# Two mirrored outputs from one weight load in the inverse transform's second stage

## The chip, the cores and the metric

One core of a Trainium2 chip runs the kernel. A NeuronCore has TensorE (PE), which multiplies a moving operand by a loaded weight and writes to PSUM; VectorE (DVE) and ScalarE (ACT), which read PSUM and write SBUF; GpSimd (POOL) and SyncE (SP), which here mostly issue transfers. The engines run side by side, each through its own instructions in order, and wait for each other by semaphores. The metric is the device time of one execution in microseconds.

## The reference

The input `x` is 8 sequences of 5696 steps with 128 channels, and `h` is one filter of the same length for each channel. The first half is a long causal convolution, computed by a Fourier transform of twice the length:

```python
Xf = np.fft.rfft(x, n=2 * S, axis=1)
Hf = np.fft.rfft(h, n=2 * S, axis=0)
y = np.fft.irfft(Xf * Hf[None], n=2 * S, axis=1)[:, :S, :]
```

The second half takes that `y` as its `x` and mixes the steps by two full 5696 x 5696 matrices:

```python
theta = x @ w_theta
zr, zi = x * np.cos(theta), x * np.sin(theta)
y = np.einsum('ts,bsd->btd', w_tok_r, zr) + np.einsum('ts,bsd->btd', w_tok_i, zi)
u = x + y
return u + np.maximum(u @ w_ch, 0.0)
```

## The kernel before

The transform of length 11392 is split into 178 x 64. Work goes in eight groups: a group is two of the sequences and one half (64) of the channels, so 128 rows in all. Each group passes four stages. Stages A and B are the forward transform and the product with the filter's spectrum, stages C and D the inverse.

- Stage A (`stage_a`, line 241): 64 matmuls of 180 columns, weights from `x` (line 250), evicted to `a_` by ACT, in group 0 and 1 in part by DVE (lines 257, 259).
- Stage B (`stage_b`, line 411): 12 chunks. Each is a block of small matmuls (`f2`, line 270), an eviction to `xs` by ACT (line 431), and a product with the filter's spectrum `hs` into `uv_t` by DVE (lines 433, 438). `hs` comes by transfers on SP (line 423), four chunks ahead.
- Stage C (`stage_c`, line 444): 16 chunks of 16 matmuls (lines 453, 454), evicted to `g_` by DVE or ACT (lines 458, 460).
- Stage D (`stage_d`, line 478): for each of 64 output columns n, 89 outputs m: a weight is a slice of `g_`, the moving operand is a slice of a table of cosines and sines, `e_t`, or of its negative, `e_neg`. The time step is 64 m + n. The result goes to `yt`, with m outermost and n innermost, in bf16, and from there to HBM.

In stage D the offset of a column from the middle is v = |n - 32|. For odd v below 28 there are 14 pairs of columns, 32 + v and 32 - v, that use the same four weights; each column of a pair takes four matmuls of 89 columns (`terms_of`, line 463). All other columns take two. That is 184 matmuls a group, in seven chunks of up to ten neighbouring columns (`CHN`, line 90). A chunk has one PSUM tile of two banks, five columns in a bank, and one eviction; chunks 0 and 3 are evicted by DVE (line 493), the other five by ACT (line 495). Columns below 32 read the table backwards (`e[:, ::-1]`, line 476).

All four stages draw their PSUM tiles from one pool of four (`psum`, line 104). The order on PE, DVE, ACT is that in which the program emits the work. A helper, `woven` (line 280), merges lists of chunks by given fractions: stage C of group g with stage A of group g + 1 (line 791), then stage D of group g with stage B of group g + 1 (line 799). In the second mix, D's seven chunks are placed from 0.08 to 1.1 and B's twelve from 0 to 0.8, so that on PE the order is B0 B1 D0 B2 B3 D1 B4 B5 B6 D2 B7 B8 D3 B9 B10 D4 B11 D5 D6. In the last group there is no stage B; five steps of the next phase (`phase_step`, line 736) stand between D's chunks. These steps compute theta, sines and cosines.

After the seventh chunk `yt` is sent off: in groups 0 to 6 by eight transfers on SP (line 502), in the last by POOL, two of them straight into the tile `ya` of the phase steps (line 729). Then come the remaining phase steps, and the mixing by the two large matrices (lines 1200 and 1279), whose weights POOL loads (line 680) and DVE transposes (line 894).

Of the kernel before, what the change touches and what calls it, by code (L numbers as in the profile page):

```python
# [15 lines left out]
AF = mybir.ActivationFunctionType  # L16
# [6 lines left out]
def kernel(  # L23
# [10 lines left out]
    nc = tc.nc  # L34
# [41 lines left out]
    N2 = 64  # L76
    N1 = NF // N2
    NB = S // N2
    K1 = N1 // 2 + 1
    CK = 8  # L80
    HD = D // 2
    EN = N2 // 2 + 1
# [3 lines left out]
    assert N1 * N2 == NF and NB * N2 == S and NB % 2 == 1 and K1 <= P  # L86
    CHK = [(c0, min(CK, K1 - c0)) for c0 in range(0, K1, CK)]
    NCK = len(CHK)
    CN = 10
    CHN = [(c0, min(CN, N2 - c0)) for c0 in range(0, N2, CN)]  # L90
    UVW = 2 * HD * K1
    YP = [(n * S // 4, (n + 1) * S // 4) for n in range(4)]
    NP = 14
    ND = N2 - 2 * NP
    RC = 2 * NP + 2 * ND
# [227 lines left out]
    ps = psum()  # L323
# [136 lines left out]
                nc.vector.tensor_copy(g_out, g_in)  # L460
        return [lambda q=q: chunk(q) for q in range(0, 2 * HD, 8)]

    def terms_of(n):

        v = abs(n - N2 // 2)
        c, s = e_t[:K1, v, 0, :], e_t[:K1, v, 1, :]
        if v % 2 and v < 2 * NP:
            i = v // 2
            c_, s_ = (e_neg[:K1, i, r, :] for r in range(2))
            late = ((s, c_) if n >= N2 // 2 else (s_, c))  # L470
            out_ = [(i, c), (NP + i, s), (RC + i, late[0]), (RC + NP + i, late[1])]
        else:
            f = (n - N2 // 2) % N2
            i = 2 * NP + (f // 2 if f % 2 == 0 else N2 // 2 + (f - 2 * NP) // 2)
            out_ = [(i, c), (ND + i, s)]
        return [(i, e if n >= N2 // 2 else e[:, ::-1]) for i, e in out_]

    def stage_d(st, bp, dh, then=None):
        def chunk(n0, cn):
            if n0 == 0:  # L480
                st["yt"] = fy.tile([P, NB, N2], BF16, tag="yt", name="yt")
            g_, yt = st["g"], st["yt"]
            ps = psum()
            nq = 5 if cn == CN else cn
            for j in range(cn):
                o = ps[:, j // nq, (j % nq) * NB:(j % nq + 1) * NB]
                terms = terms_of(n0 + j)
                for i, (at, e_) in enumerate(terms):
                    nc.tensor.matmul(o, g_[:K1, at, :], e_, start=(i == 0), stop=(i == len(terms) - 1))
            y_out = yt[:, :, n0:n0 + cn].rearrange("p m (a q) -> p m a q", q=nq)  # L490
            y_in = ps[:, :cn // nq, :nq * NB].rearrange("p a (q m) -> p m a q", q=nq)
            if n0 in (0, 3 * CN):
                nc.vector.tensor_copy(y_out, y_in)
            else:
                nc.scalar.activation(y_out, y_in, AF.Copy)
            if n0 + cn == N2:
                if then is not None:
                    then(yt)
                for t0, t1 in [(H, S)] if then else YP:
                    for e in range(2):  # L500
                        with tc.issue_after(sides["row"]) if then else ExitStack():
                            (nc.gpsimd if then else nc.sync).dma_start(
                                yt_hbm[dh * HD:(dh + 1) * HD, 2 * bp + e, t0:t1],
                                yt[64 * e:64 * e + 64].rearrange("p m n -> p (m n)")[:, t0:t1])
        return [lambda n0=n0, cn=cn: chunk(n0, cn) for n0, cn in CHN]

    zz_n, ZB = [0], 3
    groups = [(bp, dh) for bp in range(B // 2) for dh in range(2)]
# [833 lines left out]
```

## Time and profile before

| | us |
|---|---|
| median of three runs | 2044.71 (2043.49 to 2048.08) |
| the profiled execution | 2041.79 |
| its span, first to last instruction | 2040.0 |
| PE busy in the span | 1958.3 (96%) |
| DVE busy | 1538.0 (75%) |
| POOL busy | 967.4 (47%) |
| ACT busy | 640.1 (31%) |
| stage D's matmuls (line 489), one group | 184 instructions |
| stage D's evictions by DVE (line 493) | 16 x 890 elements, 1080 ns each |
| stage D's evictions by ACT (line 495) | 32 x 890 elements, 917 ns each, and 8 x 356, 448 ns |

A row of the profile gives the engine, the line of the kernel, the operation, what it writes and reads, and how often. Lengths overlap: an instruction of PE lasts about 0.2 us from its start to its modelled end, while the next one starts about 0.04 us after it, and an instruction of DVE or ACT starts some 0.1 us before the one ahead of it ends. So the cost of an instruction on a full engine is the distance to the next start, not its length. The granted clock is the share of TensorE's full clock that it was given in a stretch.

### The profile page before, as it was taken

How to read it: one execution, taken by the hardware profiler on the slowest of the kernel's cores; microseconds unless marked ns; L12 is line 12 of the kernel's file. 1: busy time of each engine (PE TensorE's matmuls, PEld its weight loads, DVE VectorE, ACT ScalarE, POOL GpSimd, SP SyncE). 2: the span in 40 equal slices, each digit the busy share in tenths (PEclk: the TensorE clock that was granted, in tenths of full speed). 3: DMA queues.
4: the chain of work that ended last, by engine and by line, in shares of the span. 5: the costliest groups of instructions: out<-in, count | busy, mean ns of one | idle time of the engine just before them, and what ended most of it. 6: DMA issues, size and time to landing. Idle time of an engine off the chain costs nothing.

```text
span 2040.0 us, 42587 instructions
## 1 busy us (share of the span) xinstructions
PE 1958.3 (96%) x16297; PEld 1080.5 (53%) x16297; DVE 1538.0 (75%) x2817; ACT 640.1 (31%) x936; POOL 967.4 (47%) x1769
## 2 busy tenths in 40 slices
PE   7899898889999999999999998999999999999998
PEld 5788897644444444444444443444444444444444
DVE  7878887657778787878776767867777786777767
ACT  6888887853233323233200000011111111111111
POOL 8324313374454545453666454453545545354450
PEclk8899999899999999999999999999999999999999
DMA  9999989899898989898999798796978869788793
GB/s 155 158 164 155 168 161 244 256 251 189 143 181 172 180 169 167 177 178 171 173 168 145 132 262 199 108 153 127 153 137 140 152 124 157 130 148 144 135 156 84
DMA packets 510349, 334.77 MB, mean 164 GB/s; under 512 B 186631, under 2 KB 463111, under 8 KB 510055
## 3 DMA queue, kind: packets, MB, share of 16 engines
q0 software_dynamic: 322368, 157.47, 60.6%
q1 hardware_dynamic: 181792, 163.03, 27.3%
q10 hardware_dynamic: 5984, 11.54, 1.6%
q8 instruction: 128, 2.10, 0.4%
q14 instruction: 77, 0.63, 0.1%
HBM read 374.82 MB, written 95.24 MB: 230 GB/s over the span
## 4 chain that ended last, share of the span: by engine, by line
PE 66%; DVE 3%; DMA 2%; issue 1%; POOL 1%; ACT 0%; DVEq 0%; ACTq 0%; SPq 0%
PE m L1279 61%; DVE c L1286 1%; DMA ring<-in_moe_w_tok_r_dram 1%; PE utp L974 1%; PE v L981 1%; PE m L1283 1%; POOL ring L680 1%; DVE b L835 1%; PE m L1166 1%; DVE wt L894 1%; DMA b<-z_hbm 1%; PE theta_ps L564 0%; PE tpz L922 0%; PE m L1200 0%; DMA zl<-zl_hbm 0%
## 5 line engine op out<-in xcount | busy, mean ns | idle before, releaser
L680 POOL DMA_DIRECT2D ring<-in_moe_w_tok_i_dram x720 | 388.5, 545 | 656.0 <-DVE wt L894 575.4
L680 POOL DMA_DIRECT2D ring<-in_moe_w_tok_r_dram x720 | 387.1, 545 | 142.9 <-DVE wt L894 83.9
L894 DVE STREAM_TRANSPOSE wt<-ring 128x384 f32<-128x384 f32 (+2 forms) x720 | 359.7, 526 | 124.6 <-PE m L1279 80.3
L1279 PE MATMUL m<-b,wt 128*128 128x512 bf16 x1640 | 389.7, 380 | 1.9 <-DVE wt L894 1.7
L1279 PEld LDWEIGHTS <-wt 128*128 128x128 bf16 x1804 | 176.3, 98 | 219.7 <-DVE wt L894 7.9
L1286 DVE TENSOR_TENSOR c<-c,m 128x512 f32<-128x512 f32 x412 | 266.4, 672 | 0.4 <-PE m L1279 0.4
L976 ACT ACTIVATE ring<-utp 128x512 bf16<-128x512 bf16 x85 | 50.8, 598 | 581.8 <-PE utp L974 581.8
L1200 PE MATMUL m<-b,wt 128*128 128x512 bf16 x480 | 113.7, 387 | 9.6 <-DMA b<-zz 3.9
L453 PE MATMUL ps<-r_u,uv_t 128*128 128x128 f16 x1024 | 118.5, 222 | 4.2 <-DVE uv_t L438 1.9
L454 PE MATMUL ps<-r_v,uv_t 128*128 128x100 f16 x1024 | 116.4, 210 | 0.1
L971 ACT ACTIVATE ub<-c 128x512 bf16<-128x512 f32 x88 | 55.2, 630 | 193.7 <-DVE c L1241 114.9
L153 POOL DMA_DIRECT2D x<-in_x_dram x128 | 99.3, 781 | 20.9 <-POOL x L151 14.9
L454 PEld LDWEIGHTS <-uv_t 128*128 128x128 f16 x1024 | 101.3, 99 | 4.6 <-issue 3.3
L453 PEld LDWEIGHTS <-uv_t 128*128 128x128 f16 x1024 | 101.6, 99 | 2.5 <-DVE uv_t L438 2.0
L433 DVE TENSOR_TENSOR uv_t<-xs,hs 128x2048 f16<-128x2048 f16 x77 | 91.2, 1223 | 14.2 <-ACT xs L431 9.4
L431 ACT ACTIVATE xs<-ps 128x1024 f16<-128x1024 f32 x96 | 90.6, 974 | 24.1 <-PE ps L270 11.0
L1200 PEld LDWEIGHTS <-wt 128*128 128x128 bf16 x528 | 51.1, 99 | 69.3 <-issue 11.0
L566 ACT ACTIVATE red<-theta_ps,magic 128x512 f32<-128x512 f32 (+1 forms) x46 | 31.7, 689 | 154.9 <-PE theta_ps L564 96.0
L270 PEld LDWEIGHTS <-w_t 64*128 64x128 f16 x3240 | 55.3, 97 | 27.1 <-issue 20.0
L924 ACT ACTIVATE ring<-tpz 128x512 bf16<-128x512 bf16 (+1 forms) x46 | 27.5, 598 | 132.2 <-PE tpz L922 118.2
L250 PE MATMUL ps<-f_t,x 89*128 89x180 f16 x512 | 65.9, 262 | 1.7 <-DVE a L257 1.6
L835 DVE TENSOR_TENSOR b<-b 128x1024 bf16<-128x1024 bf16 x100 | 61.4, 684 | 0.0
(2925 smaller groups left out, 3755.1 us busy)
## 6 DMA issues: line engine op xcount, KB each, us to landing
ring<-in_moe_w_tok_r_dram POOLq DMA_DIRECT2D x352, 96.0 KB, 4.5
ring<-in_moe_w_tok_i_dram POOLq DMA_DIRECT2D x352, 96.0 KB, 4.9
ring<-in_moe_w_tok_r_dram POOLq DMA_DIRECT2D x352, 80.0 KB, 4.5
ring<-in_moe_w_tok_i_dram POOLq DMA_DIRECT2D x352, 80.0 KB, 3.8
cp_hbm<-c SPq DMA_DIRECT2D x88, 256.0 KB, 2.6
c<-cp_hbm SPq DMA_DIRECT2D x88, 256.0 KB, 4.6
out_dram<-c SPq DMA_DIRECT2D x88, 256.0 KB, 4.2
hs<-hf_hbm SPq DMA_DIRECT2D x77, 256.0 KB, 3.7
```

The source lines that it names most:

```text
L153: nc.gpsimd.dma_start(x16[p0:p1, e, n0:n0 + 16, :HD], bass.AP(tensor=src.tensor, offset=src.offset + (p0 * N2 + n0) * D + dh * HD, ap=[[N2 ...
L250: nc.tensor.matmul(ps[:, i // 2, (i % 2) * 2 * K1:(i % 2 + 1) * 2 * K1], lhs(q + i), f1_t[:NB], start=True, stop=True)
L431: nc.scalar.activation(xs[:, :, :, :ck], ps, AF.Copy)
L433: nc.vector.tensor_tensor(uv[:, :, :, c0:c0 + ck], xs.rearrange("p e d k -> p e (d k)").unsqueeze(1).to_broadcast([P, 2, 2, HD * CK]), hv. ...
L453: nc.tensor.matmul(o, u_t[:, at:at + P], r_u, start=True, stop=False)
L454: nc.tensor.matmul(o[:, 2 * NP:], v_t[:, at:at + P], r_v, start=False, stop=True)
L680: nc.gpsimd.dma_start(wb[32 * i:32 * i + 32, :ng, :nj * 64], bass.AP(tensor=a.tensor, offset=a.offset + row0 * S + p * H + i * QR + j0 * 6 ...
L835: return [lambda f=f, x=x: f(*x) for f, x in ((nc.vector.tensor_sub, (bt[M3], b12, b22)), (nc.vector.tensor_sub, (bt[M4], b21, b11)), (nc. ...
L894: nc.vector.transpose(wt.rearrange("p j t r -> p (j t r)").bitcast(F32).rearrange("p (j g t) -> p g j t", j=TJ, g=4)[:, :ng, :nj], wb[:, : ...
L1200: nc.tensor.matmul(ms[n // 2 * 2 + h], a[n][:, j, :, r], bts_of[p][jj][n % 2 * 2 + h][:, r, :], start=(n % 2 == 0 and jj == 0 and r == 0), ...
L1279: nc.tensor.matmul(ms[q], a[q][:, j, :, r], bts[jj][q][:, r, :], start=(jj == 0 and r == 0), stop=(jj == NJ - 1 and r == 1 and q not in left))
L1286: nc.vector.tensor_tensor(c, z, ms[q], op=op)
```

## The change

The chunks of stage D are no longer neighbouring columns. `D_TILES` lists seven chunks, each with the columns of its two banks and its evictions:

- three chunks of ten even columns (0 to 18, 20 to 38, 40 to 58), as singles;
- two chunks of four pairs, and one of four pairs with the single columns 1 and 3;
- a last one with two pairs and the single columns 60 to 63.

A pair is a negative item. Its four matmuls have 178 moving columns each: for the two shared terms the same block of the table twice (a broadcast), for the two others a block and its counterpart, elsewhere in the table. The lower column of a pair then comes out with m backwards, and its eviction writes `yt` backwards (`kind` 2). Each chunk of pairs has one eviction for the upper columns and one for the lower. Singles below 32 still read the table backwards.

A group then has 72 matmuls of 89 columns and 56 of 178, and 13 evictions in place of 7: DVE has chunk 0 (890 elements) and chunk 3 (two of 356), ACT the others (two of 890, five of 356, three of 178). The chunks' places in the order are as before.

```diff
-    def terms_of(n):
-        v = abs(n - N2 // 2)
-        c, s = e_t[:K1, v, 0, :], e_t[:K1, v, 1, :]
-        if v % 2 and v < 2 * NP:
-            i = v // 2
-            c_, s_ = (e_neg[:K1, i, r, :] for r in range(2))
-            late = ((s, c_) if n >= N2 // 2 else (s_, c))
-            out_ = [(i, c), (NP + i, s), (RC + i, late[0]), (RC + NP + i, late[1])]
...
-        return [(i, e if n >= N2 // 2 else e[:, ::-1]) for i, e in out_]
+    def terms_of(item):
+        if item < 0:
+            i = ~item
+            c, s, c_, s_ = 4 * i + 2, 4 * i + 3, 2 * EN + 2 * i, 2 * EN + 2 * i + 1
+            same = [e_blk[:K1, b:b + 1, :].to_broadcast([K1, 2, NB]) for b in (c, s)]
+            return [(i, same[0]), (NP + i, same[1]), (RC + i, e_blk[:K1, s:s_ + 1:s_ - s, :]),
+                    (RC + NP + i, e_blk[:K1, c_:c - 1:c - c_, :])]
...
+    def even(k, by_dve):
+        n0 = 4 * 5 * k
+        return [list(range(n0, n0 + 10, 2)), list(range(n0 + 10, n0 + 20, 2))], [(by_dve, 0, 2, 0, 5, 0, n0, 2)]
+
+    def pairs_of(k, by_dve, more=()):
+        i = 4 * k
+        banks = [[~i, ~(i + 1), *more[:1]], [~(i + 2), ~(i + 3), *more[1:]]]
+        return banks, [(by_dve, 0, 2, 0, 2, 1, H_ + 1 + 2 * i, 2), (by_dve, 0, 2, 0, 2, 2, H_ - 1 - 2 * i, -2),
+                       *([(by_dve, 0, 2, 4 * NB, 1, 0, more[0], 2)] if more else [])]
+
+    D_TILES = [even(0, True), pairs_of(0, False), even(1, False), pairs_of(1, True), pairs_of(2, False, (1, 3)), even(2, False),
+               ([[~12, ~13], list(range(N2 - 4, N2))],
+                [(False, 0, 1, 0, 2, 1, H_ + 25, 2), (False, 0, 1, 0, 2, 2, H_ - 25, -2), (False, 1, 1, 0, 4, 0, N2 - 4, 1)])]
...
     def stage_d(st, bp, dh, then=None):
-            for j in range(cn):
-                o = ps[:, j // nq, (j % nq) * NB:(j % nq + 1) * NB]
-                terms = terms_of(n0 + j)
-                for i, (at, e_) in enumerate(terms):
-                    nc.tensor.matmul(o, g_[:K1, at, :], e_, start=(i == 0), stop=(i == len(terms) - 1))
-            y_out = yt[:, :, n0:n0 + cn].rearrange("p m (a q) -> p m a q", q=nq)
-            y_in = ps[:, :cn // nq, :nq * NB].rearrange("p a (q m) -> p m a q", q=nq)
-            if n0 in (0, 3 * CN):
+            for bank, items in enumerate(banks):
+                at = 0
+                for item in items:
+                    w = 2 * NB if item < 0 else NB
+                    o = ps[:, bank, at:at + w]
+                    if item < 0:
+                        o = o.rearrange("p (h m) -> p h m", h=2)
+                    terms = terms_of(item)
+                    for k, (col, e_) in enumerate(terms):
+                        nc.tensor.matmul(o, g_[:K1, col, :], e_, start=(k == 0), stop=(k == len(terms) - 1))
+                    at += w
+            for by_dve, bank, nb, at, nq, kind, n0, dn in evictions:
+                y_in = ps[:, bank:bank + nb, at:at + nq * NB * (2 if kind else 1)]
+                n1 = n0 + dn * nb * nq
+                y_out = yt[:, ::-1, n0:n1:dn] if kind == 2 else yt[:, :, n0:n1:dn]
...
+                if by_dve:
                     nc.vector.tensor_copy(y_out, y_in)
```

More of the change, by code (lines that the diff above doesn't have):

```diff
@@ L88 @@
     NCK = len(CHK)
-    CN = 10
-    CHN = [(c0, min(CN, N2 - c0)) for c0 in range(0, N2, CN)]
     UVW = 2 * HD * K1
@@ L309 @@
     e_t = e_flat.rearrange("p (n r m) -> p n r m", r=2, m=NB)
+    e_blk = e_all.rearrange("p (b m) -> p b m", m=NB)
     e_f = [e_flat[:K1, 22 * NB * n:22 * NB * (n + 1)].bitcast(F32) for n in range(3)]
@@ L461, in stage_c @@
         return [lambda q=q: chunk(q) for q in range(0, 2 * HD, 8)]
-    def terms_of(n):
-        v = abs(n - N2 // 2)
-        c, s = e_t[:K1, v, 0, :], e_t[:K1, v, 1, :]
-        if v % 2 and v < 2 * NP:
-            i = v // 2
-            c_, s_ = (e_neg[:K1, i, r, :] for r in range(2))
-            late = ((s, c_) if n >= N2 // 2 else (s_, c))
-            out_ = [(i, c), (NP + i, s), (RC + i, late[0]), (RC + NP + i, late[1])]
[L472 to L475, printed above, removed]
-        return [(i, e if n >= N2 // 2 else e[:, ::-1]) for i, e in out_]
+    def terms_of(item):
[5 more added lines that the diff above has]
+                    (RC + NP + i, e_blk[:K1, c_:c - 1:c - c_, :])]
+        v = abs(item - N2 // 2)
+        f = (item - N2 // 2) % N2
+        i = 2 * NP + (f // 2 if f % 2 == 0 else N2 // 2 + (f - 2 * NP) // 2)
+        return [(at, e_t[:K1, v, r, :] if item >= N2 // 2 else e_t[:K1, v, r, ::-1])
+                for r, at in ((0, i), (1, ND + i))]
@@ new lines @@
+    H_ = N2 // 2
+    def even(k, by_dve):
[6 more added lines that the diff above has]
+                       *([(by_dve, 0, 2, 4 * NB, 1, 0, more[0], 2)] if more else [])]
@@ L478, in stage_d, with chunk @@
+    D_TILES = [even(0, True), pairs_of(0, False), even(1, False), pairs_of(1, True), pairs_of(2, False, (1, 3)), even(2, False),
+               ([[~12, ~13], list(range(N2 - 4, N2))],
+                [(False, 0, 1, 0, 2, 1, H_ + 25, 2), (False, 0, 1, 0, 2, 2, H_ - 25, -2), (False, 1, 1, 0, 4, 0, N2 - 4, 1)])]
+    assert NP == 14
     def stage_d(st, bp, dh, then=None):
-        def chunk(n0, cn):
-            if n0 == 0:
+        def chunk(n_, banks, evictions):
+            if n_ == 0:
                 st["yt"] = fy.tile([P, NB, N2], BF16, tag="yt", name="yt")
@@ L483, in chunk @@
             ps = psum()
-            nq = 5 if cn == CN else cn
-            for j in range(cn):
-                o = ps[:, j // nq, (j % nq) * NB:(j % nq + 1) * NB]
-                terms = terms_of(n0 + j)
-                for i, (at, e_) in enumerate(terms):
-                    nc.tensor.matmul(o, g_[:K1, at, :], e_, start=(i == 0), stop=(i == len(terms) - 1))
-            y_out = yt[:, :, n0:n0 + cn].rearrange("p m (a q) -> p m a q", q=nq)
-            y_in = ps[:, :cn // nq, :nq * NB].rearrange("p a (q m) -> p m a q", q=nq)
-            if n0 in (0, 3 * CN):
[L493 to L496, printed above, removed]
+            for bank, items in enumerate(banks):
[13 more added lines that the diff above has]
+                y_out = yt[:, ::-1, n0:n1:dn] if kind == 2 else yt[:, :, n0:n1:dn]
+                y_out = y_out.rearrange("p m (a q) -> p m a q", q=nq)
+                if kind:
+                    y_in = y_in.rearrange("p a (q h m) -> p m a q h", h=2, m=NB)[:, :, :, :, kind - 1]
+                else:
+                    y_in = y_in.rearrange("p a (q m) -> p m a q", m=NB)
+                if by_dve:
+                    nc.vector.tensor_copy(y_out, y_in)
+                else:
+                    nc.scalar.activation(y_out, y_in, AF.Copy)
+            if n_ + 1 == len(D_TILES):
                 if then is not None:
@@ L504, in chunk @@
                                 yt[64 * e:64 * e + 64].rearrange("p m n -> p (m n)")[:, t0:t1])
-        return [lambda n0=n0, cn=cn: chunk(n0, cn) for n0, cn in CHN]
+        return [lambda n_=n_, t=t: chunk(n_, *t) for n_, t in enumerate(D_TILES)]
     zz_n, ZB = [0], 3
```

## The prediction

> **What bounds the kernel now.** I read four views, in this order: the table by stage, the timeline of one group's end, the clock by gate windows, and the groups by line. In each fence below a line of the table by stage is: window, its length, then busy time (and instructions) of PE, PE weight load, DVE, ACT, POOL, the granted clock, DMA.
>
> The stages first. The first two windows are one group of the transform (its D/B stretch, in which stage D of one group is mixed with stage B of the next, then its C/A stretch); the last is all of the mixing.
>
> ```profile
> 201.90:220.00 18.10, 15.47 (x555) 14.32 (x553) 16.47 (x16) 15.12 (x18) 4.88 (x9) 1.00 0.93 152
> ...
> 220.00:237.80 17.80, 17.77 (x313) 17.54 (x312) 13.17 (x12) 15.31 (x21) 8.47 (x16) 1.00 1.28 181
> ...
> 400.00:2040.00 1640.00, 1613.51 (x8505) 766.12 (x8502) 1226.28 (x2434) 325.36 (x531) 813.15 (x1502) 0.99 0.87 161
> ```
>
> The mixing is 1640 of the 2040 us, and the change has no instruction in it. The edited stage lies in eight stretches before 381 us: seven D/B stretches of about 18 us and one last D stretch (366.8 to 381.2 us). In D/B it is DVE that is full (16.47 of 18.10 us), with PE waiting in between; in C/A it is PE (17.77 of 17.80). So whatever D does to PE counts only at the seams of D/B, and in the last stretch, where phase steps take B's place.
>
> The seam is in the timeline (start, length, engine, line, what, count).
>
> ```profile
> 215.72 0.38 PE L270 MATMUL ps<-a__4565,w_t 64*128 64x64 f16 x13 [0.66 <-issue]
> 216.03 1.28 PEld L489 LDWEIGHTS <-g__4578 90*128 90x128 f16 x30
> 216.24 1.08 DVE L493 CAST yt<-ps 128x890 bf16<-128x890 f32 x1
> 217.24 2.36 DVE L433 TENSOR_TENSOR uv_t<-xs,hs 128x2048 f16<-128x2048 f16 x2
> 217.38 0.29 PE L270 MATMUL ps<-a__4565,w_t 64*128 64x64 f16 x8
> 217.49 0.93 ACT L495 ACTIVATE yt<-ps 128x890 bf16<-128x890 f32 x1
> 217.60 1.62 PEld L489 LDWEIGHTS <-g__4578 90*128 90x128 f16 x38
> 218.55 0.41 ACT L431 ACTIVATE xs<-ps 128x256 f16<-128x256 f32 x1
> 219.07 1.27 ACT L495 ACTIVATE yt<-ps 128x890 bf16<-128x890 f32 x2
> 219.17 0.69 PEld L250 LDWEIGHTS <-x 89*128 89x128 f16 x8
> 219.50 0.71 DVE L438 TENSOR_TENSOR uv_t<-xs,hs 128x256 f16<-128x256 f16 x2
> 219.97 0.10 PEld L453 LDWEIGHTS <-uv_t 128*128 128x128 f16 x1
> ```
>
> See three chains meet within 0.3 us of 219.97, where C begins: DVE's last product (L438), PE's own row D5, D6, A (216.03 to about 219.8 almost without a break), and ACT's eviction of D5 (219.07), which frees the PSUM tile for C. No one of them can be shortened alone to gain more than that.
>
> **The change part by part.** Matmul spacing: 30 weight loads of D in 1.28 us, the last lasting 0.10: (1.28 - 0.10)/29 = 41 ns per 89 columns. The nearest row for 178 columns is L250, 180 columns with a weight load each: (0.69 - 0.16)/7 = 76 ns; I take 77. Below: 74 (a mixing matmul of 512 columns takes about 215 ns in the chain, 18 in 3.88 us, 0.42 ns per column, 75 for 178). Above: 2 x 41 = 82, no gain.
> - PE per group: before 184 x 41 = 7.54 us. After: 14 pairs of 4 matmuls at 77 and 36 single columns of 2 at 41: 4.31 + 2.95 = 7.26. That is 0.28 us less (0 to 0.45). The weight loads that go (56) were already under the matmuls before them: PE was spaced by columns, and the columns stay 16,376 per group.
> - By chunk, D0 to D6, PE was 26, 30, 30, 30, 30, 30, 8 matmuls: 1.07, 1.23 (five times), 0.33 us. After: 20 singles 0.82; 16 pairs 1.23; 0.82; 1.23; 16 pairs and 4 singles 1.40; 0.82; 8 pairs and 8 singles 0.94. So D0 to D2 get 0.66 us lighter and D4 to D6 0.37 heavier.
> - DVE per group: before two casts of 890, each holding the engine 1.00 us (216.24 to 217.24). After one of 890 and two of 356. There is no row for 356 on DVE; casts of 720 (L257) last 0.90 against 1.08, 1.05 ns an element, so 1.00 - 534 x 0.00105 = 0.44 each, from 0.40 (pure scaling) to 0.50 (no gain): 0.12 us less (0 to 0.2).
> - ACT per group: two evictions in 1.27 us at 219.07, of 890 and 356 elements; the 356 alone lasts about 0.45, so the 890 holds ACT 0.82. The 356 of the last group starts at 380.67 and the next instruction at 381.01: 0.34. That gives 0.9 ns an element, and 0.18 for 178. Before 4 x 0.82 + 0.34 = 3.62; after five of 356, two of 890, three of 178: 1.70 + 1.64 + 0.54 = 3.88, 0.26 us more, nearly all in D6 (0.34 to 0.70). Waits and semaphores of five more instructions are in these spacings.
> - The write patterns are new: every second 2-byte element, and mirrored ones backwards. Price zero by the nearest row, stage A's eviction (L259), which writes 4 elements and jumps: 720 in 0.77 us against 1024 contiguous in 1.02 (L431), the same rate within 0.1 us. The upper end is twice the time; that is a rival below. [...]
> - The moving operands (a block twice, or two blocks apart, no longer reversed for the lower half) have no row of their own: reversed and straight D matmuls are now both spaced 40 to 42 ns, so zero. No DMA, queue or wait is moved: yt still leaves after the seventh chunk, for all four quarters, by SP (by POOL in the last group).
>
> The seam, per group. DVE's chain ends 0.12 earlier. PE's row: in groups 1, 4 and 5 it pauses 0.9 to 1.3 us after D4, which hides D4's growth, so the row grows by D5 + D6, 1.76 for 1.56, and was 0.2 early: C starts about 0.07 earlier. In groups 2 and 3 D4 runs straight into the last f2, the row grows by 0.37 less the 0.2 slack: about 0.13 later. Group 0 ends at half clock (below) and its row is on the path: about 0.4 later. Group 6 ends in a wait for something else. Then ACT enters C/A 0.3 us behind; it has 2.5 us to spare there (15.31 of 17.80). Sum of the seven: -0.2 + 0.26 + 0.4 = about +0.5 us.
> The last stretch: PE is 0.28 lighter; but yt's last eviction (380.67 to 381.17) releases the POOL transfer at 381.46, whose landing 6.5 us later is what PE waits for until 388.6. D6's matmuls begin 0.6 earlier and take 0.6 longer, and ACT has 0.43 more from D4 on, against 0.5 that DVE's and PE's earlier D3 give: -0.1 to +0.4, I take 0.
> Sum: +0.5 us on the profiled 2041.8 (span 2040.0 and 1.8 around it). That execution lies 2.9 us under the median of the runs, 2044.7; with half a microsecond added that is 2045.2, and I say 2045. The ends of the forecast, all terms at their bounds: 7 x -0.25 - 0.45 = -2.2, and 7 x 0.4 + 0.8 = +3.6.
>
> **The rivals.**
> - The clock gate (slower). The granted clock falls to half after a window of 3.41 us in which PE did little:
>
> ```profile
> 102.36:105.77 3.41, 2.05 (x62) 1.97 (x62) 3.39 (x4) 2.97 (x4) 0.00 (x0) 1.00 0.62 179
> 105.77:109.18 3.41, 3.07 (x45) 2.97 (x45) 3.15 (x5) 1.90 (x4) 0.00 (x0) 0.50 0.55 149
> 109.18:112.60 3.42, 3.42 (x33) 3.42 (x32) 0.31 (x1) 2.37 (x4) 0.00 (x0) 0.50 0.84 239
> 208.17:211.59 3.42, 2.32 (x90) 2.07 (x82) 2.75 (x4) 2.45 (x3) 0.00 (x0) 1.00 1.06 218
> ```
>
>  In the fourth line 2.32 us busy kept full speed; it holds D2, which loses 0.41 us of PE work. 2.32 - 0.41 = 1.91 is under the 2.05 of the first line, after which the clock fell. Group 0 with its two half windows took 21.9 + 18.4 us (88.5 to 110.4 to 128.8) where group 3 took 18.1 + 17.8: up to 4 us, some of it start-up; a single fall I put at 1 to 2. From three more falls in the seven groups it decides: +3 x 1.5 + 0.5, 2050. Against it: D4 and D6 get denser, 365.18 to 368.60 was busy 1.81 us and kept its clock, and DVE's pace hides part of a slow PE. [...]
> - The strided writes are slow (slower). If stepping costs as much again, DVE has 1.9 us more and ACT 3.9 in each D/B stretch, and DVE's is on the path: 7 x 1.9 + 1.5 in the last, about +15, 2060. Only the row of stage A speaks against it.
> - PSUM turnover, not DVE, paces D/B (faster). D0 to D2 free PSUM tiles and PE 0.66 us sooner, and f2 (L270) waits for tiles of D behind yt evictions; if all of it is gained in seven groups, with 0.28 in the last, and group 0 keeps its clock (2): -4.9 + -2 at most, say -5, 2040. Against it, DVE has only 1.6 us of idle time per stretch, part of it for hs's DMA.
> - The change does nothing at all for PE: 178 columns cost 82 ns. That is +0.28 per group on PE, inside the forecast.
>
> **How the numbers follow.** 0.2% (4.1 us) is about what a measurement of this kernel can tell from no change. Forecast (within it) 0.50. Gate 0.20 and strided writes 0.06, both slower; small losses at all seams together beyond 0.2%, 0.02: slower 0.28. PSUM turnover, faster, 0.22. For 8 in 10 the range goes from the faster rival's 2040 to near the gate's 2050: 2040 to 2049.5. The forecast's own range is 2042.5 to 2048.3.
>
> **What would show it.** D's wide matmuls 76 to 78 ns apart, 128 per group; ACT's 178 and 356 evictions lasting about 0.30 and 0.45 us, DVE's 356 about 0.52; C starting within 0.2 us of before, relative to the start of its group, and the D/B windows 17.6 to 18.5 us; the wait for ya ending near 388.6. Wrong would be: evictions twice as long (writes), half-clock windows in groups 1 to 5 (gate), or D/B stretches of 17.5 us and less (PSUM turnover).

## The result, and the profile after

The changed kernel takes 2052.89 us (median of 10 runs, 2050.11 to 2057.68); the kernel before, beside it, 2046.05 (10 runs, 2035.21 to 2054.95). The ratio is put at 1.0048, with a 95% interval of 1.0031 to 1.0064; the quotient of the two medians, 1.0033, lies near the lower end of it. So the change makes the kernel slower by some 7 (medians) to 10 us (ratio), where the forecast was no measurable difference, at 2045, and the range ended at 2049.5.

The page's head for the kernel after: span, then busy time, share of the span and number of instructions of each engine.

```profile
span 2053.3 us, 41565 instructions
...
PE 1945.1 (95%) x15673; PEld 1076.2 (52%) x15849; DVE 1540.2 (75%) x2825; ACT 654.0 (32%) x976; POOL 967.8 (47%) x1769
```

This profiled execution took 2055.04 us, 1.7 us of it outside the span. It is a rather long one of its ten, and the profiled one of before (2041.8) a rather short one, so the two spans lie 13.3 us apart, more than the medians. What follows looks for where those 13.3 us are, and judges the causes by the medians.

The source view of stage D's matmul shows when each group's stage D begins. The columns are line, engine, tiles, count, then least/median/longest duration in ns, then the first and the last start in us. Before:

```profile
L489 PE MATMUL ps<-e_t,g__1416 x184: 200/204/283, 90.1 to 109.2; 90*128 90x89 f16 x184
...
L489 PE MATMUL ps<-e_t,g__5629 x184: 201/203/218, 239.3 to 255.4; 90*128 90x89 f16 x184
L489 PE MATMUL ps<-e_t,g__6680 x184: 201/203/218, 275.6 to 290.8; 90*128 90x89 f16 x184
L489 PE MATMUL ps<-e_t,g__7730 x184: 200/204/283, 311.0 to 329.9; 90*128 90x89 f16 x184
L489 PE MATMUL ps<-e_t,g__8861 x184: 201/203/208, 366.8 to 379.9; 90*128 90x89 f16 x184
```

After:

```profile
L508 PE MATMUL ps<-e_t,g__1416 x128: 201/239/355, 90.2 to 110.3; 90*128 90x89 f16 x72, 90*128 90x178 f16 x56
...
L508 PE MATMUL ps<-e_t,g__5429 x128: 201/206/251, 245.9 to 262.7; 90*128 90x89 f16 x72, 90*128 90x178 f16 x56
L508 PE MATMUL ps<-e_t,g__6430 x128: 201/206/251, 283.7 to 300.3; 90*128 90x89 f16 x72, 90*128 90x178 f16 x56
L508 PE MATMUL ps<-e_t,g__7430 x128: 201/239/354, 321.3 to 340.2; 90*128 90x89 f16 x72, 90*128 90x178 f16 x56
L508 PE MATMUL ps<-e_t,g__8511 x128: 201/205/243, 377.5 to 391.3; 90*128 90x89 f16 x72, 90*128 90x178 f16 x56
```

From one group's first matmul to the next one's it took 36.3 and 35.4 us before (275.6 - 239.3, 311.0 - 275.6), and 37.8 and 37.6 after. These groups ran at full clock (the longest duration is 251 ns or less; it is 283 before and 354 or 355 after in the first and the seventh group, which have a stretch at half clock). The first stage D begins alike (90.1 and 90.2), the seventh 10.3 us and the last one 10.7 us later: over the first six groups this is a loss of 1.7 us a group.

The table by stage splits one such period at the first matmul of stage C. The windows begin at the first matmul of stage D, 1.5 us later than the prediction's, so a D/B stretch is shorter here than there. As in the prediction, a line is the window, its length, busy time and instructions of PE, weight load, DVE, ACT, POOL, then clock, DMA share and GB/s. Before, the D/B and the C/A stretch of the group that begins at 203.4:

```profile
203.40:220.00 16.60, 14.30 (x488) 13.33 (x489) 15.25 (x15) 13.98 (x17) 3.61 (x6) 1.00 0.96 162
220.00:239.30 19.30, 18.93 (x377) 18.54 (x377) 14.39 (x13) 16.45 (x22) 9.74 (x19) 1.00 1.24 170
```

After, the same two:

```profile
208.00:226.00 18.00, 14.55 (x433) 13.15 (x434) 15.68 (x16) 14.92 (x20) 3.58 (x6) 1.00 0.89 160
226.00:245.90 19.90, 19.20 (x376) 18.64 (x376) 14.27 (x12) 17.12 (x24) 9.76 (x19) 1.00 1.16 156
```

D/B is 1.4 us longer (cut in the same way, over six groups 1.2 on average) and C/A 0.6. In D/B no engine is fuller than before: PE has 3.45 us left, DVE 2.3, ACT 3.1. So the time went into waits between them. At full clock D/B took 16.1 to 17.5 us before (five stretches, mean 16.80) and 17.7 to 18.0 after (three, mean 17.85). In C/A, ACT has 0.67 us more to do.

The groups by line show what each eviction of stage D cost after the change (count, then busy us and mean ns of one, then idle time ahead).

```profile
L522 ACT ACTIVATE yt<-ps 128x890 bf16<-128x890 f32 x16 | 22.4, 1398 | 0.3 <-PE ps L508 0.3
L522 ACT ACTIVATE yt<-ps 128x356 bf16<-128x356 f32 x40 | 21.1, 581 | 2.4 <-PE ps L508 2.4
L522 ACT ACTIVATE yt<-ps 128x178 bf16<-128x178 f32 x24 | 12.9, 627 | 0.4 <-PE ps L508 0.4
...
L520 DVE CAST yt<-ps 128x890 bf16<-128x890 f32 x8 | 10.8, 1347 | 2.1 <-PE ps L508 2.1
L520 DVE CAST yt<-ps 128x356 bf16<-128x356 f32 x16 | 7.9, 546 | 0.0
```

An eviction of 890 elements that writes every second column takes ACT 1.40 us; before the change one of 890 neighbours took 0.92 (29.4 us for 32). DVE's takes 1.35, before 1.08; DVE's 356 elements, in rows of four, take 0.55. And 178 elements, two stepped columns, take as long as 356 (627 and 581 ns). ACT's evictions of stage D add up to 56.4 us, where they were 33.1 before (29.4, and 3.7 for the eight of 356, which take 461 ns on average; the 448 in the table of before is the shortest): 23.3 us more.

PE did what the change says. Sixteen wide matmuls run in 1.42 us, the last lasting 0.24: (1.42 - 0.24)/15 is 79 ns apart, against 41 for one of 89 columns ((0.98 - 0.20)/19). The timeline after, start and length first:

```profile
208.00 0.98 PE L508 MATMUL ps<-e_t,g__4428 90*128 90x89 f16 x20 [0.36 <-DVE g__4428 L459]
...
210.09 1.42 PE L508 MATMUL ps<-e_t,g__4428 90*128 90x178 f16 x16
```

Two places of the same D/B stretch show the loss, again in the timeline after:

```profile
217.32 1.38 ACT L522 ACTIVATE yt<-ps 128x890 bf16<-128x890 f32 x1
...
218.54 1.92 ACT L430 ACTIVATE xs<-ps 128x1024 f16<-128x1024 f32 x2
...
219.59 2.36 DVE L432 TENSOR_TENSOR uv_t<-xs,hs 128x2048 f16<-128x2048 f16 x2 [0.90 <-ACT xs L430]
...
224.48 2.55 ACT L522 ACTIVATE yt<-ps 128x890 bf16<-128x890 f32 x4
...
225.98 0.22 PE L452 MATMUL ps<-r_u,uv_t 128*128 128x128 f16 x1 [0.24 <-ACT yt L522]
...
226.88 0.80 ACT L257 ACTIVATE a__5416<-ps 128x720 f16<-128x720 f32 x1
```

In these rows ACT's instructions run one behind the other. The first place is its eviction of D2 (217.32 to 218.70). Behind it, without a gap, stands the eviction of B7 to `xs` (218.54), and DVE, whose next product needs it, waits 0.90 us until it is done (219.59). In the kernel before, the same three instructions, and stage C's first matmul, are

```profile
212.11 0.91 ACT L495 ACTIVATE yt<-ps 128x890 bf16<-128x890 f32 x1
...
212.90 1.95 ACT L431 ACTIVATE xs<-ps 128x1024 f16<-128x1024 f32 x2
213.97 2.36 DVE L433 TENSOR_TENSOR uv_t<-xs,hs 128x2048 f16<-128x2048 f16 x2 [0.38 <-ACT xs L431]
...
220.04 0.22 PE L453 MATMUL ps<-r_u,uv_t 128*128 128x128 f16 x1
```

Here DVE waits 0.38 us. The second place is the end. Stage C's first matmul (225.98) waits 0.24 us for a tile that ACT still evicts; before the change this wait was 0.02 us. DVE's last products are not late on their own: in both kernels they follow the product ahead of them without a pause. At the start of stage C, ACT then has 1.05 us of D's evictions left (224.48 + 2.55 - 225.98) before its first for stage A, at 226.88. Before the change it had 0.30 left (219.07 + 1.27 - 220.04; the first two are in the prediction's lines). That is 0.7 us of backlog carried into C/A, about what C/A grew.

The last stretch, after:

```profile
394.81 0.89 ACT L522 ACTIVATE yt<-ps 128x178 bf16<-128x178 f32 x2
...
395.99 1.06 POOL L756 DMA_DIRECT2D ya<-yt  x2 [25.32 <-ACT yt L522]
...
404.18 0.59 PE L776 MATMUL tpz<-ident_bf,ya 128*128 128x128 bf16 x4 [4.94 <-ACT cos L619]
```

From the first matmul of the last stage D to the matmul that ends PE's long wait it is 26.7 us (404.18 - 377.5), before 21.8 (388.6 - 366.8). Before the change, the last transfer into `ya` and ACT's last cosine ahead of that matmul both end within 0.1 us of its start. After the change `ya` is complete at 403.1 (issued at 396.5, 6.5 us to landing), and PE waits 1.1 us more for ACT's cosine, as the row says. At that point the kernel is 15.6 us behind, 10.7 and 4.9; by the end 13.3. The rest of the execution takes 1649.1 us, and 1651.4 before; in the profiles of the timed experiments below it takes 1647.0 to 1654.9, so these 2.3 us are within the scatter of single executions.

### The profile page after: what moved, and what is told of

Read it like the earlier page. It is cut to its first block, busy times and chain, and to the rows that moved or that the text cites. A ratio compares the mean times of both kernels' runs of the same rounds, so it can differ in the third digit from the quotient of the medians.

```text
span 2053.3 us, 41565 instructions
## 1 busy us (share of the span) xinstructions
PE 1945.1 (95%) x15673; PEld 1076.2 (52%) x15849; DVE 1540.2 (75%) x2825; ACT 654.0 (32%) x976; POOL 967.8 (47%) x1769
## 4 chain that ended last, share of the span: by engine, by line
PE 63%; DVE 4%; DMA 3%; POOL 2%; issue 2%; ACT 0%; DVEq 0%; ACTq 0%; POOLq 0%
PE m L1306 59%; POOL ring L707 2%; DVE c L1313 1%; DMA ring<-in_moe_w_tok_r_dram 1%; PE utp L1001 1%; PE v L1008 1%; DVE b L862 1%; PE m L1310 1%; DVE wt L921 1%; DMA b<-z_hbm 1%; PE theta_ps L591 0%; PE tpz L949 0%; DMA wl<-in_moe_w_tok_i_dram 0%; PE m L1193 0%; DMA zl<-zl_hbm 0%
## 5 line engine op out<-in xcount | busy, mean ns | idle before, releaser
L707 POOL DMA_DIRECT2D ring<-in_moe_w_tok_i_dram x720 | 388.6, 546 | 656.8 <-DVE wt L921 581.2
L1306 PE MATMUL m<-b,wt 128*128 128x512 bf16 x1605 | 386.5, 380 | 3.7 <-DVE wt L921 1.7
L1227 PE MATMUL m<-b,wt 128*128 128x512 bf16 x471 | 111.8, 383 | 8.0 <-DMA b<-zz 3.3
L151 POOL DMA_DIRECT2D x<-in_x_dram x128 | 98.1, 772 | 20.5 <-POOL x L149 14.9
L432 DVE TENSOR_TENSOR uv_t<-xs,hs 128x2048 f16<-128x2048 f16 x77 | 91.7, 1220 | 18.1 <-ACT xs L430 10.5
```

Source lines behind the costliest of these rows:

```text
L151: nc.gpsimd.dma_start(x16[p0:p1, e, n0:n0 + 16, :HD], bass.AP(tensor=src.tensor, offset=src.offset + (p0 * N2 + n0) * D + dh * HD, ap=[[N2 ...
L432: nc.vector.tensor_tensor(uv[:, :, :, c0:c0 + ck], xs.rearrange("p e d k -> p e (d k)").unsqueeze(1).to_broadcast([P, 2, 2, HD * CK]), hv. ...
L707: nc.gpsimd.dma_start(wb[32 * i:32 * i + 32, :ng, :nj * 64], bass.AP(tensor=a.tensor, offset=a.offset + row0 * S + p * H + i * QR + j0 * 6 ...
L1227: nc.tensor.matmul(ms[n // 2 * 2 + h], a[n][:, j, :, r], bts_of[p][jj][n % 2 * 2 + h][:, r, :], start=(n % 2 == 0 and jj == 0 and r == 0), ...
L1306: nc.tensor.matmul(ms[q], a[q][:, j, :, r], bts[jj][q][:, r, :], start=(jj == 0 and r == 0), stop=(jj == NJ - 1 and r == 1 and q not in left))
```

## The experiments

The theory after the result: the stepped writes alone make the kernel slower. Its rivals: the new grouping (other PSUM tiles, another order, thirteen evictions a group for seven); the wide matmuls; the clock gate. Each comparison below is against the kernel before, run on the same chip.

**The step without the rest.** In the kernel before, six chunks are written two columns apart; matmuls, tiles and the number of evictions stay.

```diff
-            y_out = yt[:, :, n0:n0 + cn].rearrange(...)
+            at = n0 if cn < CN else n0 // (2 * CN) * 2 * CN + n0 // CN % 2
+            y_out = yt[:, :, at:at + (cn if cn < CN else 2 * CN - 1):1 if cn < CN else 2].rearrange(...)
```

> The kernel before with one thing changed: the six chunks of ten columns are written two columns apart in yt (chunks 0 and 1 interleaved, 2 and 3, 4 and 5) in place of side by side, so the outputs stand at permuted time steps. Matmuls, chunk order, number and size of evictions are those of before. Theory W (the stepped writes cost the time): ACT's evictions of 890 elements last 1.35 to 1.4 us as in the changed kernel (0.92 before), DVE's 1.35 (1.08), and the time rises by 7 to 16 us, ratio 1.0035 to 1.008. Rival N (13 evictions in place of 7, and the heavier last chunks, cost it): no more than 2 us, ratio 0.999 to 1.001. Rival M (the wide matmuls cost it): as N.

Measured: 2050.69 us, ratio 1.0044 (1.0028 to 1.0059). The groups by line of this kernel:

```profile
L496 ACT ACTIVATE yt<-ps 128x890 bf16<-128x890 f32 x32 | 44.5, 1390 | 9.2 <-PE ps L489 7.0 <-DMA hs<-hf_hbm 2.2
L494 DVE CAST yt<-ps 128x890 bf16<-128x890 f32 x16 | 21.6, 1349 | 2.6 <-PE ps L489 2.6
L496 ACT ACTIVATE yt<-ps 128x356 bf16<-128x356 f32 x8 | 3.7, 466 | 0.0
```

The stepped evictions have the durations of the changed kernel, the one that is left contiguous has that of before (0.47), and the whole loss is there without a wide matmul or a new grouping.

**The rest without the step.** The changed kernel, with the even columns in the first half of `yt` and the odd ones in the second, so that every eviction writes neighbours.

```diff
-                y_out = yt[:, ::-1, n0:n1:dn] if kind == 2 else yt[:, :, n0:n1:dn]
+                p0, step = n0 // 2 + n0 % 2 * (N2 // 2), dn // 2
+                p1 = p0 + step * nb * nq
+                y_out = yt[:, ::-1, p0:p1:step] if kind == 2 else yt[:, :, p0:p1:step]
...
```

> The changed kernel with one thing changed: yt is laid out with the 32 even columns first and the 32 odd ones behind them, so that each of the 13 evictions writes neighbours (the mirrored ones still backwards); the outputs stand at permuted time steps. Theory W: evictions of 890 last 0.92 us on ACT again, 1.08 on DVE, of 356 about 0.45, of 178 about 0.30, and the time is that of before or up to 3 us less, ratio 0.9985 to 1.001. Rivals N and M: as the changed kernel, 1.003 to 1.0065.

Measured: 2041.14 us, ratio 0.9997 (0.9985 to 1.0008). The groups by line:

```profile
L529 ACT ACTIVATE yt<-ps 128x890 bf16<-128x890 f32 x16 | 14.4, 903 | 0.3 <-PE ps L508 0.3
L529 ACT ACTIVATE yt<-ps 128x356 bf16<-128x356 f32 x32 | 13.4, 467 | 2.4 <-PE ps L508 2.4
...
L529 ACT ACTIVATE yt<-ps 128x178 bf16<-128x178 f32 x24 | 7.2, 340 | 0.9 <-PE ps L508 0.9
```

With 3.9 us for the eight evictions of the last four columns, ACT's sum is 38.9 us. So of ACT's 23.3 us more, 17.5 (56.4 - 38.9) are the step and 5.8 (38.9 - 33.1) the larger number of evictions, and the 5.8 cost the kernel nothing that can be measured (the interval ends at +0.08%, 1.6 us). Together the two runs settle it: the step is enough, and nothing else of the change is needed for the loss.

The last stretch is an exception in the small. Here too it is longer than before, 25.4 us for 21.8 (391.12 - 365.7), so 3.6 of its 4.9 us belong to the grouping, whose last chunk has three evictions for one among the sines and cosines on ACT. The step alone adds the other 1.3: in the kernel with the step and nothing else it is 23.1 (395.95 - 372.8). This kernel is 2.5 us behind at that point and 0.2 at the end of its span, a difference within the scatter named above.

**The change with narrow matmuls.** Each pair takes two times four matmuls of 89 columns again; the grouping and the stepped writes stay.

```diff
-                    for k, (col, e_) in enumerate(terms):
-                        nc.tensor.matmul(o, g_[:K1, col, :], e_, start=(k == 0), stop=(k == len(terms) - 1))
+                    for h in range(2 if item < 0 else 1):
+                        for k, (col, e_) in enumerate(terms):
+                            oh, eh = (o[:, h, :], e_[:, h, :]) if item < 0 else (o, e_)
+                            nc.tensor.matmul(oh, g_[:K1, col, :], eh, start=(k == 0), stop=(k == len(terms) - 1))
```

> The changed kernel with the widening undone: each pair is again two times four matmuls of 89 columns, so 184 a group; chunks and the 13 evictions as in the changed kernel. Theory W: like the changed kernel, 0 to 3 us more, ratio 1.0035 to 1.007. Rival M: back at the time of before, 0.999 to 1.001. Rival N: as W.

Measured: 2049.1 us, ratio 1.0039 (1.0027 to 1.0052), within the interval of the changed kernel. The widening is not what makes it slower, and no gain of it is seen either.

**What a stepped write costs.** The kernel before, with extra evictions of the first chunk, repeated in all eight groups; for the durations alone.

```diff
+                nc.scalar.activation(two(at(yt, 10, 1)), in10, AF.Copy)
+                nc.scalar.activation(two(at(yt, 10, 2)), in10, AF.Copy)
+                nc.scalar.activation(two(at(yt, 10, 4)), in10, AF.Copy)
+                nc.scalar.activation(two(at(yt, 10, 6)), in10, AF.Copy)
+                nc.scalar.activation(two(at(y32, 10, 1)), in10, AF.Copy)
...
```

> The kernel before with 19 more evictions of the first chunk of stage D in each group, into columns that are overwritten later, for their lengths alone (the time rises by some 100 us): ACT and DVE, 10, 4 and 2 columns a row, bf16 at a step of 1, 2, 4 and 6 elements, and fp32 side by side. If what counts is that two neighbours share a 4-byte word, bf16 at steps 2, 4 and 6 all last about 1.38 us on ACT for 890 elements, and fp32 side by side too. If what counts is how many 16-byte pieces a row touches (2 at step 1, 3 at step 2, 5 at step 4, 8 at step 6), the time grows with the step, and fp32 side by side (3 pieces) is like step 2. If it is the sub-word write at a step, fp32 stays at 0.92 us.

The source view of the added lines on ACT, in this order from the second on (steps of 2, 4 and 6 columns in bf16; neighbours in fp32); durations are least/median/longest:

```profile
L502 ACT ACTIVATE yt<-ps x8: 1359/1368/1373, 92.7 to 491.5; 128x890 bf16<-128x890 f32 x8
L503 ACT ACTIVATE yt<-ps x8: 2100/2123/2144, 94.1 to 493.2; 128x890 bf16<-128x890 f32 x8
L504 ACT ACTIVATE yt<-ps x8: 2845/2892/2962, 96.2 to 495.7; 128x890 bf16<-128x890 f32 x8
L505 ACT ACTIVATE yt<-ps x8: 912/912/932, 99.1 to 498.9; 128x890 f32<-128x890 f32 x8
```

Neighbours in bf16 took 923 ns. So it is not the bytes: fp32 side by side writes twice as many in the same time (912). And it is not a single price for a step: it grows with the distance (1368, 2123 and 2892 ns for steps of 2, 4 and 6). On DVE the steps 1, 2 and 4 took 1085, 1348 and 2101.

**Whose evictions count.** The kernel before, once with only ACT's chunks 1, 2, 4 and 5 stepped, once with only DVE's 0 and 3.

```diff
-            y_out = yt[:, :, n0:n0 + cn].rearrange(...)
+            at, by = ((0, 1), (20, 2), (21, 2), (10, 1), (40, 2), (41, 2), (60, 1))[n0 // CN]
+            y_out = yt[:, :, at:at + by * (cn - 1) + 1:by].rearrange(...)
```

> The kernel before with only ACT's chunks 1, 2, 4 and 5 written two columns apart (1 and 2 interleaved, 4 and 5), DVE's two chunks side by side; outputs at permuted time steps. If it is ACT's evictions that carry the loss (theory A): most of the 9 us of the run with all six stepped, ratio 1.0025 to 1.005. If DVE, the fuller engine of the D/B stretches, carries it (theory D): ratio 1.000 to 1.002.

The other one has the table `((0, 2), (20, 1), (30, 1), (1, 2), (40, 1), (50, 1), (60, 1))`.

> The kernel before with only DVE's chunks 0 and 3 written two columns apart (interleaved with each other), ACT's side by side; outputs at permuted time steps. DVE has 2 x 0.27 us more in each of seven D/B stretches, 3.8 us in all. Theory D: ratio 1.0018 or more. Theory A: 0.999 to 1.001.

Measured: ACT's alone 2051.15 us, ratio 1.0053 (1.0032 to 1.0073); DVE's alone 2042.8, 1.0011 (0.9994 to 1.0027), which lies between the ranges of the two theories. ACT's 15 us of stepping (32 times 0.47) are enough for the whole loss; of DVE's 4.3 us (16 times 0.27) between nothing and all could be on the path.

The timelines show how the loss comes about. The table takes the D/B stretches at full clock of the groups from the second to the sixth: their number and mean length, DVE's wait for the `xs` that ACT evicts behind D2, and the wait of stage C's first matmul for a tile.

| kernel | stretches | D/B, us | DVE waits, us | PE waits, us |
|---|---|---|---|---|
| before | 5 | 16.80 | 0.38 to 0.71 | 0.01 to 0.02 |
| after | 3 | 17.85 | 0.89 to 0.90 | 0.24 to 0.26 |
| after, narrow | 3 | 17.68 | 0.72 to 0.91 | 0.20 to 0.23 |
| step alone | 2 | 17.80 | 0.44 and 0.89 | 0.51 |
| ACT's step alone | 4 | 17.69 | 0.86 to 1.29 | 0.52 to 0.53 |
| DVE's step alone | 3 | 16.86 | 0.48 to 0.49 | 0.02 |
| after, neighbours | 4 | 16.74 | 0 to 0.50 | 0 |

Where ACT's evictions are stepped, C's first matmul waits and D/B is 0.9 to 1.05 us longer, and DVE's wait is longer in all stretches but one; where they are not, all three are about as before. In these three stretches DVE's step adds 0.06 us of the 0.54 that it takes DVE.

**Wide matmuls with neighbours in the true layout.** If the step is the cause, a tile that holds four neighbouring columns above the middle and the four mirrored ones below should do without it: two pairs and four single columns, an upper run and a lower run, each written as neighbours. Seven such tiles and one with the last eight columns, which DVE evicts; DVE also has tiles 0 and 3.

```diff
+    def run_tile(k, by_dve):
+        v = 4 * k
+        banks = [[H_ + v + 2 * b, ~(2 * k + b), H_ - v - 2 * b - 2] for b in range(2)]
+        return banks, [(by_dve, H_ + v, 1), (by_dve, H_ - v - 1, -1)]
...
+    D_TILES = [run_tile(k, k in (0, 3)) for k in range(7)] + [([list(range(N2 - 4, N2)), list(range(4))], None)]
...
+                y_in = ps[:, :2, 2 * NB * lo:2 * NB * lo + 2 * NB].rearrange("p a (q m) -> p m a q", m=NB)
+                y_out = yt[:, ::-1, n0:n0 - 4:-1] if lo else yt[:, :, n0:n0 + 4]
...
```

> The wide matmuls with evictions that write neighbours, output as in the reference: eight chunks; seven of them hold four columns just above the middle and four just below (two pairs and four singles), each with two evictions of four neighbouring columns, and the last holds columns 60 to 63 and 0 to 3. DVE has chunks 0, 3 and the last, ACT the others. Evictions of 356 last 0.46 us on ACT, 0.52 on DVE; the last two stand in DVE's pause of 1 us before stage C's first eviction. Theory W (only the steps cost): the time of before or up to 5 us less, 0.9975 to 1.0005. Rival N (the number of evictions, 16 here): 1.001 to 1.004.

Measured: 2040.55 us, ratio 0.9992 (0.9973 to 1.0011). The loss is gone with the output's own layout. But no gain: the waits from 88 to 330 us show PE held up by DVE's evictions in this kernel,

```profile
PE ps L268 <- DVE yt L512: 7.9, 11, 1.4
```

against 3.4 us in 4 times before.

**More patterns.** The kernel before with further extra evictions: other steps in fp32 and bf16, an odd start, backwards, pairs of neighbours in every four columns, and one column of 89 elements alone.

```diff
+                nc.scalar.activation(two(at(y32, 10, 3)), in10, AF.Copy)
+                nc.scalar.activation(two(at(yt, 10, 3)), in10, AF.Copy)
+                nc.scalar.activation(yt[:, :, 0:20].rearrange("p m (q c) -> p m q c", c=4)[:, :, :, 0:2], in5, AF.Copy)
+                nc.scalar.activation(y32[:, :, 0:1], ps[:, 0, :NB].rearrange("p (m o) -> p m o", o=1), AF.Copy)
+                nc.scalar.activation(yt[:, :, 0:1], ps[:, 0, :NB].rearrange("p (m o) -> p m o", o=1), AF.Copy)
...
```

> As the first probe, other patterns. On ACT the 890 elements took 0.92, 1.37, 2.12, 2.89 us at bf16 steps of 1, 2, 4, 6 and 0.91 in fp32 side by side. If the time goes with the bytes from one element to the next unless they touch: fp32 at a step of 2 (8 bytes) 2.1, at 3 (12 bytes) 2.9, bf16 at a step of 3 (6 bytes) 1.75. If it goes with the step in elements: fp32 at 2 1.37, at 3 1.75. Pairs of bf16 neighbours every four columns: 0.92 if touching pairs are enough, 1.37 if the bytes covered count. Backwards by one, at an odd start, and without a gap between rows: 0.92 each.

The source view of those five, in this order (fp32 by 3, bf16 by 3, pairs of neighbours, one column in fp32, one column in bf16):

```profile
L505 ACT ACTIVATE yt<-ps x8: 1299/1317/1331, 91.3 to 464.5; 128x890 f32<-128x890 f32 x8
L506 ACT ACTIVATE yt<-ps x8: 1656/1727/1756, 92.6 to 466.2; 128x890 bf16<-128x890 f32 x8
...
L511 ACT ACTIVATE yt<-ps x8: 914/975/986, 98.2 to 473.8; 128x890 bf16<-128x890 f32 x8
L512 ACT ACTIVATE yt<-ps x8: 318/328/335, 99.2 to 474.8; 128x89 f32<-128x89 f32 x8
L513 ACT ACTIVATE yt<-ps x8: 565/567/567, 99.5 to 475.1; 128x89 bf16<-128x89 f32 x8
```

Pairs of touching bf16 elements with gaps between the pairs cost almost nothing (975 ns for 923); single ones do (1368 to 2892). In fp32 a step of 2 took 1016 and of 3 1317, for 912 side by side: a step costs there too, but less at the same distance in bytes (at 8 bytes 1016, for 2123 in bf16). Backwards took 914, so the mirrored order was rightly priced at zero. Neighbours that begin at an odd column took 1094, where 0.92 us had been expected.

**DVE out of the way.** The run tiles, with tile 3 evicted by ACT.

```diff
-    D_TILES = [run_tile(k, k in (0, 3)) for k in range(7)] + ...
+    D_TILES = [run_tile(k, k == 0) for k in range(7)] + ...
```

> The kernel with runs of four neighbours (e7), with chunk 3 evicted by ACT in place of DVE, so that DVE has 0.9 us less in each D/B stretch and ACT 0.7 more. f2 waited 7.9 us in all for DVE's evictions in e7. If DVE's place in the chain is what bounds D/B: ratio to the kernel before 0.996 to 0.9985. If ACT does, as the runs with stepped writes on one engine alone say: 0.9985 to 1.002.

Measured: 2034.07 us (2029.79 to 2036.88), ratio 0.9956 (0.9937 to 0.9975). This is faster than both kernels. The waits from 88 to 330 us now have

```profile
PE ps L268 <- DVE yt L512: 1.3, 4, 0.3
```

so with a smaller share of the evictions on DVE, PE hardly waits for them. Part of the gain came with the clock: over whole executions its mean was 0.987 here, 0.984 in the run tiles and 0.985 in the kernel before, and among the 25 executions of the kernel before that were run beside the first experiments, those with a mean lower by 0.01 took about 11 us more.

**Is that the run tiles at all?** The kernel before, with chunk 3 given to ACT and the small chunk 6 to DVE.

```diff
-            if n0 in (0, 3 * CN):
+            if n0 in (0, 6 * CN):
```

> The kernel before with two evictions exchanged between the engines and nothing else: chunk 3 (890 elements) goes from DVE to ACT and chunk 6 (356) from ACT to DVE, where DVE has a pause. DVE 0.6 us less in a D/B stretch, ACT 0.5 more. DVE-bound: 0.9965 to 0.999. ACT-bound: 1.000 to 1.003.

Measured: 2037.56 us, ratio 0.9979 (0.9961 to 0.9996). About half of that gain is to be had by moving an eviction from DVE to ACT alone; the 3.4 us in which PE waited for DVE's evictions between 88 and 330 us are gone from its trace. The rest belongs to the run tiles: the two kernels were run beside each other, twelve times each, with medians 3.5 us apart, and ten executions of the run tiles took 2035.0 us or less, where three of this kernel did.

**And of the widening?** The run tiles with tile 3 on ACT, pairs as two times four matmuls of 89 again (the edit of the narrow kernel above).

> The best version so far (e9: runs of four neighbours, chunk 3 by ACT) with the widening undone: each pair is two times four matmuls of 89 columns, the rest as in e9. If the wide matmuls are worth something once the writes cost nothing: 0.1% or more above e9's 0.9956, ratio 0.9966 to 0.999. If they are worth nothing, since PE is not what bounds these stretches: 0.994 to 0.9965.

Measured: 2036.33 us, ratio 0.9976 (0.9963 to 0.9989). By the expectation this speaks for the widening. But the interval overlaps that of the wide form, 0.9937 to 0.9975, the two were not run beside each other, and the quotients of the medians are 0.9974 here and 0.9969 there. In the changed kernel the narrow form was ahead by 0.1%. Whether the widening is worth anything stays open, and it is at most a few us.

Across the kernels, from single profiles: the six group periods (first to seventh start of stage D, source view) and the ratio.

| kernel | six periods, us | ratio |
|---|---|---|
| before | 311.0 - 90.1 = 220.9 | 1 |
| after | 321.3 - 90.2 = 231.1 | 1.0048 |
| step alone | 318.3 - 89.1 = 229.2 | 1.0044 |
| after, neighbours | 310.5 - 88.5 = 222.0 | 0.9997 |
| after, narrow | 318.6 - 89.4 = 229.2 | 1.0039 |
| ACT's step alone | 314.5 - 88.7 = 225.8 | 1.0053 |
| DVE's step alone | 313.7 - 89.4 = 224.3 | 1.0011 |
| run tiles | 316.4 - 89.9 = 226.5 | 0.9992 |
| run tiles, tile 3 on ACT | 303.8 - 89.0 = 214.8 | 0.9956 |
| before, chunks swapped | 306.8 - 89.8 = 217.0 | 0.9979 |
| run tiles, narrow | 307.3 - 89.1 = 218.2 | 0.9976 |

The periods of a single execution have a scatter of several us, from the half-clock windows that it happens to have: the run tiles had 37.5 us of them between 85 and 345 us, before 10.2. The three kernels in which both engines' evictions are stepped stand out all the same (229.2 and more); for ACT's step alone the stretches at full clock, above, say more than this sum.

## Why the prediction was wrong

**The step that failed is the price of the write patterns.** The prediction said "Price zero by the nearest row, stage A's eviction (L259), which writes 4 elements and jumps". That row was not near: its four elements touch, and touching elements cost next to nothing extra even in pairs (975 ns for 0.92 us). Single bf16 elements, two apart, cost 0.47 us more for 890 on ACT (1390 ns for 917) and 0.27 on DVE (1349 for 1080), and more the further apart (2123 ns on ACT and 2101 on DVE at four). ACT's term of the sum was +0.26 us a group; it measured 23.3/8 = 2.9, of which 2.2 are the step and 0.7 the additional evictions. DVE's was -0.12; the step alone adds 0.27 + 2 x 0.02 = 0.3 to it, most of it in the eviction of 890 (1347 ns for 1080; 356 in rows of four lose 0.02 us in the first probe, 547 ns for 529).

**The rival that came true is the strided writes, at a chance of 0.06.** Its direction and its place (D/B) were right. It asked for twice the time, +15 us; the step of two costs half as much again on ACT and a quarter on DVE, and the kernel lost 7 to 10. It put the loss on DVE, "on the path". The runs with one engine stepped show it on ACT: ACT's step alone is the whole loss, and DVE's alone at most 0.27%. By the full engine of the stage table DVE had seemed the bound and ACT's 3.0 us of idle time (15.12 of 18.10) a cover. But ACT's eviction of D2 stands directly ahead of the `xs` that DVE waits for (0.9 us for 0.4 to 0.7), and its last evictions hold the tile that stage C needs (0.24 us for 0.02), so ACT's extra time is passed on although ACT is idle elsewhere in the stretch. Beside the step's 17.5 us on ACT the kernel lost 7 to 10 us: roughly half arrived in the time.

The 16-byte pieces that a row touches, the second guess ahead of the first probe, do not set these losses by themselves: in bf16 at a step of 2 four elements fall into 16 bytes and ACT loses 0.45 us (1368 ns for 923), at 4 two do and 1.20 us are lost (2123), but in fp32 a step of 2, which also puts two elements into 16 bytes, loses 0.10 (1016 for 912).

**The seams.** "C starting within 0.2 us of before" failed: D/B grew by 1.2 us a group on average (1.05 at full clock), and C/A, which was to have 2.5 us to spare on ACT, by 0.6. The last goes with three stepped evictions at the end of stage D. With the step but one contiguous eviction in the last chunk C/A was 19.1 us, with three contiguous ones 19.4, with three stepped ones 19.9, wide or narrow (19.3 before). That the backlog on ACT is what links the two is read from the timeline, and was not tried by itself.

**The last stretch.** Forecast -0.1 to +0.4, measured +4.9, of which 3.6 come without the step, from the grouping, and 1.3 from the step. This was a second miss, in the term for ACT, which has the sines and cosines to do between the evictions. The prediction took the landing of `ya` for the end of PE's wait; in the changed kernel ACT's cosine ends it, 1.1 us later. The kernel without the step, which has the 3.6 us too, shows no net loss; what makes up for them was not followed.

**What was right.** The wide matmuls came 79 ns apart for the 77 taken (76 to 78 had been named), and no gain in time was seen from it, in a stretch where PE is idle for 3.45 us of 18. The backward write cost nothing (914 ns for 923).

**The other rivals.** The clock gate (0.20): the changed kernel has 20.5 us at half clock between 85 and 345 us, before 10.2; in the one the clock fell four times, in the other twice, each time behind 3.41 us in which PE was busy for 0.55 to 2.05. But the kernel with only DVE's chunks stepped has 20.5 and loses nothing that can be told, the one with ACT's has 13.7 and loses most, and the periods from 245.9 to 321.3 us lose 1.5 and 2.2 us at full clock. Over whole executions the mean granted clock was 0.9856 in the changed kernel (ten), 0.9874 in its narrow form (eleven), which lost too, and 0.9854 in the kernel before (25, beside the first experiments). So the gate is not the cause of the loss. With ACT's step alone and with the step alone it was 0.984, which by the 11 us for 0.01 named above is 2 us of their loss at most. PSUM turnover (0.22) would have shown in the kernel with neighbours, which keeps D0 to D2 light: 0.9997. That the change does nothing for PE (82 ns) is nearly so: 79 ns leave it 0.17 us a group (56 times 3 ns), and nothing of that is seen in the time.

The evidence was at hand to put more on the strided rival: the prediction itself called the patterns new, had no row of single 2-byte elements, and the bound "twice the time" was within a factor of two of the loss. It was the chance of 0.06, not the bound, that left it out of the range.

## What to carry to other kernels

When an output is regrouped, look first at how many neighbouring elements each eviction writes: here a price for "strided" taken from runs of four did not hold for single 2-byte elements (1.40 us on ACT for 890 of them, 0.92 for neighbours). The regrouping could be done so that runs of touching elements stay, even mirrored ones: the run tiles are at 0.9992 and 0.9956 of the time before. And an engine that was idle for a sixth of a stretch (ACT, 3.0 us of 18.1) was no cover for longer work that stood, in its order, ahead of what the full engine waited for (0.9 us for 0.4 to 0.7).

## What the runs showed of the hardware that was not expected

- Writing bf16 from PSUM to every k-th element of SBUF: 890 elements took ACT 0.92, 1.37, 1.73, 2.12 and 2.89 us for k of 1, 2, 3, 4 and 6, about 0.4 us more for each step; DVE 1.08, 1.35, 1.69 and 2.10 for 1 to 4.
- fp32 into the same tile: ACT 0.91, 1.02 and 1.32 us for k of 1, 2, 3, DVE 1.07, 1.08 and 1.28. So at 8 bytes from element to element bf16 takes 2.12 us and fp32 1.02; a column of 89 elements by itself takes 567 ns in bf16 and 328 in fp32.
- Two touching bf16 elements in every four took ACT 0.98 us and DVE 1.07; neighbours from an odd start took ACT 1.09. Why single 2-byte elements are so much dearer than pairs stays open: the runs show the sizes, not the mechanism.
